# A fused attention and FFN kernel on one core: the opening phase rebuilt, steps spread by time, the global values product in one matmul

## The chip, the core and the metric

The kernel runs on one NeuronCore of one Trainium2 chip. The metric is the device time of one execution in microseconds (us); the time before is 426.11 us, the median of three runs (425.46 to 426.5). The engines are called as the profile calls them: PE is TensorE (matmuls; PEld is its weight load), DVE is VectorE, ACT is ScalarE, POOL is GpSimd, SP is SyncE. PE writes its results to PSUM[...]; DVE and ACT read them from there into SBUF. DMAs are issued from SP and from POOL. Each engine runs its own instructions in the order in which the program issues them, and waits for the other engines by semaphores.

## The reference

Eight batches of eight heads, 576 tokens, 64 values a head. Attention with a window of 32 tokens to each side and eight global tokens that see, and are seen by, every token; then a gated FFN over all 4608 tokens:

```python
scores = scale * np.matmul(q, k.transpose(0, 1, 3, 2))
mask = (np.abs(pos[:, None] - pos[None, :]) <= 32) | is_global[:, None] | is_global[None, :]
attn = softmax(np.where(mask, scores, -1e9))            # over the last axis
x = np.matmul(attn, v).transpose(0, 2, 1, 3).reshape(4608, 512)
g = x @ w_gate                                          # 512 -> 1536
out = (g * sigmoid(g) * (x @ w_val)) @ w_out            # 1536 -> 512
```

All inputs and the output are float32 in HBM; inside the kernel the matmuls take bf16.

## The kernel before

**Attention of one batch** (`attention(b)`) is a list of sixteen small groups of steps. `step_T(hp)` transposes keys and queries of two heads on PE (lines 274 to 296), ACT copies the keys from PSUM to `kT`, DVE the queries to `qT`. `step_GT` transposes the gathered global rows (`kqm`). `step_S2` and `step_SG` are the scores of the global queries and of the global keys, with the mask tables `mg2` and `mg` multiplied in on DVE; `step_P2T` and `step_AV2` give the result rows of the global queries, which DVE turns into the operand `gvt`. `step_S(u)` computes the scores of a band of 128 keys by 64 queries for two or four heads, ACT takes the exponential (line 396), DVE multiplies by `band` (line 401). `step_AV(u)` multiplies the probabilities by the values, for two blocks of 128 tokens: into each PSUM tile `ps_av` go a global part (line 427) and eight local products of 64 queries each (line 437). The local products of the odd half blocks need `vb`, a copy of the values moved by 64 partitions, which SP makes by two DMAs from `va` to `vb` (lines 97 to 101). `normalise` (lines 408 to 417, three DVE instructions) divides by the sum and writes `xa`. `step_X(tp)` transposes `xa` back, and ACT copies the result to `xT`, the FFN's input.

**The FFN** (`ffn(c)`) goes by chunks of 512 tokens, nine in all. `gate(fc)`, twelve times, makes two groups of four matmuls into the PSUM tiles `pg` and `pv` (line 525), a tanh on ACT (line 531), and two products on DVE (lines 533 and 536), the last of which writes `h`. `outp(ts)`, four times, makes twelve matmuls into `po` (line 541); ACT scales it to `osb`, and SP stores that.

**The order of the work** is written out by hand. First come the loads and tables, then the whole of `attention(0)`, then nine chunks; after the i-th of the sixteen units of chunk c stands the i-th group of `attention(c+1)`. After the third unit stands `prefetch(c+2)`: gather, queries and keys, values and `gather_mask` of a later batch, all issued by POOL. POOL's queue at the start is: keys and queries of heads 0 to 3, constants, heads 4 to 7, more constants and clears of `va`, the gather, the five value loads, `gather_mask(0)`, six loads of gate and value weights (512 KB each as written), `prefetch(1)`, four loads of the output weights.

**PSUM**: tag `sc` (two banks, one buffer) holds scores; tag `m` (two buffers of one bank) holds `ps_t`, `ps_g`, `ps_p2t`, `ps_av`, `ps_x`; tag `f` (four buffers of one bank) holds `pg`, `pv`, `po`.

Of the kernel before, what the change touches and what calls it, by code (L numbers as in the profile page):

```python
# [17 lines left out]
P = 128  # L18
# [8 lines left out]
def kernel(  # L27
# [22 lines left out]
    NCH = NT // CH  # L50
# [23 lines left out]
    def load_qk_part(b, tiles, hg):  # L74
        for name, src in (("k", k), ("q", q)):
            nc.gpsimd.dma_start(  # L76
                out=tiles[name][:, 4 * hg : 4 * hg + 4, :],
                in_=src[b, 4 * hg : 4 * hg + 4].rearrange("h (p j) d -> p h (j d)", j=LJ),
            )
# [6 lines left out]
    va_bufs = [const.tile([P, 5, H, W], BF16, name=f"va{i}") for i in range(2)]  # L86

    def load_v(b):
        va = va_bufs[b % 2]
        vs = v[b].rearrange("h s d -> s h d")  # L90
        for u in range(5):
            lo = WIN if u == 0 else 0
            hi = P - WIN if u == 4 else P
            t0 = P * u - WIN
            nc.gpsimd.dma_start(out=va[lo:hi, u, :, 0:D], in_=vs[t0 + lo : t0 + hi])  # L95

    def load_vb(b):
# [11 lines left out]
    load_qk_part(0, loaded[0], 0)  # L109
# [4 lines left out]
    iq_i = const.tile([P, KC], I32)  # L114
    nc.gpsimd.iota(iq_i, pattern=[[1, KC]], base=-WIN, channel_multiplier=0)
    load_qk_part(0, loaded[0], 1)
    i8_i = const.tile([P, NG], I32)
    nc.gpsimd.iota(i8_i, pattern=[[1, NG]], base=0, channel_multiplier=0)
    bofs_i = const.tile([P, B], I32)
    nc.gpsimd.iota(bofs_i, pattern=[[H * S, B]], base=0, channel_multiplier=0)  # L120
    band = const.tile([P, 64], BF16)
    nc.gpsimd.memset(band, 1.0)
    nc.gpsimd.affine_select(
        out=band, in_=band, compare_op=ALU.is_ge, fill=0.0,
        base=0, pattern=[[-1, 64]], channel_multiplier=1,
    )
    nc.gpsimd.affine_select(
        out=band, in_=band, compare_op=ALU.is_ge, fill=0.0,
        base=2 * WIN, pattern=[[1, 64]], channel_multiplier=-1,
    )  # L130
    for i in range(2):
        nc.gpsimd.memset(va_bufs[i][:, :, :, D : D + 2], 0.0)
        nc.gpsimd.memset(va_bufs[i][:, :, :, D : D + 1], 1.0)
        nc.gpsimd.memset(va_bufs[i][0:WIN, 0, :, :], 0.0)
        nc.gpsimd.memset(va_bufs[i][P - WIN : P, 4, :, :], 0.0)


    gidx_f = const.tile([P, NG], FP32)
    nc.vector.tensor_copy(
        out=gidx_f, in_=gidx_i64.bitcast(I32).rearrange("p (a b) -> p a b", b=2)[:, :, 0]  # L140
# [4 lines left out]
    )  # L145
    tmp8 = const.tile([P, NG], FP32)
# [3 lines left out]
    oh16 = const.tile([P, HP, 2, 2], FP32)  # L150
    nc.vector.tensor_reduce(
        out=oh16.rearrange("p h a r -> p (h a r)"),
        in_=ident.rearrange("p (a g) -> p a g", g=NG), axis=AX.X, op=ALU.add,
    )
    dmask = const.tile([P, HP, 2], FP32)
    nc.vector.tensor_tensor(out=dmask, in0=oh16[:, :, 0, :], in1=oh16[:, :, 1, :], op=ALU.add)
    mka = const.tile([P, 2, 2], FP32)
    nc.vector.tensor_reduce(
        out=mka, in_=oh16.rearrange("p h a r -> p a r h"), axis=AX.X, op=ALU.add
    )  # L160
    asel = const.tile([P, 2], FP32)
    nc.vector.tensor_reduce(out=asel, in_=mka, axis=AX.X, op=ALU.add)
    i8_f = const.tile([P, NG], FP32)
    nc.vector.tensor_copy(out=i8_f, in_=i8_i)
# [9 lines left out]
    bofs_f = const.tile([P, B], FP32)  # L174
    nc.vector.tensor_copy(out=bofs_f, in_=bofs_i)
    nc.vector.tensor_scalar(out=gofs, in0=bofs_f, scalar1=hrow, scalar2=None, op0=ALU.add)

# [21 lines left out]
    kqms = [None] * B  # L199
    g0 = gather(0)  # L200
    load_v(0)
    kqms[0] = gather_mask(*g0)
# [14 lines left out]
    for i in range(3):  # L217
        load_wgv(i)


    iq = const.tile([P, KC], FP32)
    nc.vector.tensor_copy(out=iq, in_=iq_i)
    nc.vector.tensor_scalar(out=iq, in0=iq, scalar1=gcol, scalar2=None, op0=ALU.subtract)
    m1 = const.tile([P, KC], BF16)
    nc.vector.tensor_scalar(out=m1, in0=iq, scalar1=0.0, scalar2=None, op0=ALU.is_equal)
    m0 = const.tile([P, KC], BF16)
    nc.vector.tensor_tensor(out=iq, in0=iq, in1=iq, op=ALU.mult)
    nc.vector.tensor_scalar(
        out=m0, in0=iq, scalar1=(WIN + 0.5) ** 2, scalar2=None, op0=ALU.is_gt
    )  # L230
    ones = const.tile([P, P], BF16)
    nc.vector.memset(ones, 1.0)
    ps_i = psc.tile([P, 2, 512], FP32, tag="sc", name="ps_i")
    for i in range(2):
        nc.tensor.matmul(
            out=ps_i[:, i, 0:320], lhsT=ones, rhs=m1[:, 320 * i : 320 * (i + 1)],
            start=True, stop=True,
        )
    mg = const.tile([P, S], BF16)
    mt = const.tile([P, KC], BF16)  # L240
    nc.vector.tensor_scalar(
        out=mg, in0=m0[:, WIN : WIN + S], scalar1=asel[:, 0:1], scalar2=None, op0=ALU.mult
    )
    nc.vector.scalar_tensor_tensor(
# [324 lines left out]
    for s in attention(0):  # L569
        for f in s:  # L570
            f()
# [40 lines left out]
```

The softmax here doesn't subtract the row's maximum and nothing guards it: scores larger than these inputs give would overflow.

## Time and profile before

| What | Value |
|---|---|
| Median of three runs | 426.11 us |
| The profiled execution, its own time | 426.5 us |
| Its span from first to last instruction | 424.5 us |
| PE busy | 377.0 us, 89% of the span |
| DVE busy | 266.2 us, 63% |
| ACT busy | 178.7 us, 42% |
| POOL busy | 92.7 us, 22% |
| First matmul of the first FFN chunk | 43.95 us |
| First matmul of the second chunk | 91.61 us |
| From chunk to chunk, second to seventh | 44.46 us |
| First matmul of the eighth chunk (no attention left) | 358.38 us |

Busy time is summed over instructions of an engine; the idle time before an instruction is put down to what released it. The modelled end of a matmul lies some tenths of a microsecond behind the time at which the next may start, so that distances between starts are the better measure on PE. The span is cut into three: the opening to 43.95 us, seven chunks that carry the attention of the next batch, and two chunks of FFN alone.

### The profile page before, as it was taken

The numbers are of one execution on the slowest core, as the hardware profiler recorded it, in microseconds if no ns is written. First come the engines' busy times: TensorE is split into PE (matmuls) and PEld (weight loads), VectorE is DVE, ScalarE is ACT, GpSimd is POOL, SyncE is SP. The second block draws the span as 40 slices with busy tenths as digits, with TensorE's granted clock in tenths as the row PEclk, the third lists the DMA queues.
The fourth block names the chain that finished last, engine by engine and source line by source line (L and its number), as shares of the span: only waits on it lengthen the run. The fifth ranks groups of instructions, "written<-read, shape, count | busy, mean of one in ns | idle before, by whom it ended". The sixth has DMA issues, their size and how long they took to land.

```text
span 424.5 us, 9105 instructions
## 1 busy us (share of the span) xinstructions
PE 377.0 (89%) x3788; PEld 192.4 (45%) x3850; DVE 266.2 (63%) x583; ACT 178.7 (42%) x281; POOL 92.7 (22%) x134
## 2 busy tenths in 40 slices
PE   0467888999989998999899989999999989999996
PEld 0345444444544444454454445445444544444442
DVE  5456488727872788267845795488628882761760
ACT  1153255345643464256524653356245633323321
POOL 8942848232015101312113211100000000000000
PEclk9999999999999999999999999999999999999999
DMA  7999999883537273647355726500030002002002
GB/s 112 68 199 208 183 212 149 109 142 57 82 23 123 73 110 23 100 92 113 23 76 116 112 18 71 124 2 2 27 121 6 2 2 100 0 2 99 0 2 99
DMA packets 62234, 33.76 MB, mean 80 GB/s; under 512 B 39409, under 2 KB 56305, under 8 KB 62193
## 3 DMA queue, kind: packets, MB, share of 16 engines
q0 software_dynamic: 55584, 19.40, 40.6%
q1 hardware_dynamic: 6608, 13.77, 9.7%
q8 instruction: 30, 0.49, 0.5%
q14 instruction: 12, 0.09, 0.1%
HBM read 38.28 MB, written 9.44 MB: 112 GB/s over the span
## 4 chain that ended last, share of the span: by engine, by line
PE 69%; DVE 19%; ACT 5%; issue 3%; POOL 2%; DVEq 0%; ACTq 0%; POOLq 0%
PE po L541 22%; PE pg L525 17%; PE pv L525 16%; DVE pt L401 5%; PE ps_t L282 5%; DVE xa L414 3%; DVE h L536 3%; DVE gv L533 3%; ACT pe L396 3%; PE ps_x L468 2%; DVE den L413 2%; PE ps_av L427 1%; ACT kT L288 1%; DVE gvt L365 1%; PE ps_av L437 1%
## 5 line engine op out<-in xcount | busy, mean ns | idle before, releaser
L533 DVE SCALAR_TENSOR_TENSOR gv<-th,pg 128x512 bf16<-128x512 bf16 x108 | 74.0, 685 | 61.4 <-ACT th L531 54.4
L525 PE MATMUL pv<-xT,wv_sb 128*128 128x512 bf16 x418 | 109.7, 381 | 0.4
L525 PE MATMUL pg<-xT,wg_sb 128*128 128x512 bf16 x400 | 106.7, 382 | 3.4 <-issue 2.6
L541 PE MATMUL po<-wo_sb,h 128*128 128x512 bf16 x416 | 97.3, 380 | 0.8
L531 ACT ACTIVATE th<-pg 128x512 bf16<-128x512 f32 x108 | 64.5, 598 | 69.3 <-PE pg L525 65.0
L536 DVE TENSOR_TENSOR h<-gv,pv 128x512 bf16<-128x512 bf16 x108 | 74.3, 688 | 11.9 <-PE ps_s L388 0.5
L525 PEld LDWEIGHTS <-wv_sb 128*128 128x128 bf16 x432 | 42.5, 98 | 51.6 <-issue 1.1
L541 PEld LDWEIGHTS <-h 128*128 128x128 bf16 x432 | 40.2, 98 | 45.3
L95 POOL DMA_DIRECT2D va<-in_v_dram x40 | 33.8, 852 | 122.6 <-PE ps_av L437 90.4
L546 ACT ACTIVATE osb<-po 128x512 f32<-128x512 f32 x36 | 21.5, 597 | 89.5 <-PE po L541 89.5
L525 PEld LDWEIGHTS <-wg_sb 128*128 128x128 bf16 x432 | 36.1, 98 | 38.2 <-issue 4.1
L396 ACT ACTIVATE pe<-ps_s 128x1024 bf16<-128x1024 f32 (+1 forms) x40 | 37.6, 940 | 15.4 <-PE ps_s L388 13.9
L410 DVE TENSOR_REDUCE den<-ps_av 128x4 f32<-128x8 f32 x72 | 11.5, 159 | 41.1 <-PE ps_av L457 34.4
L288 ACT COPY kT<-ps_t 128x576 bf16<-128x576 bf16 x32 | 20.4, 638 | 36.8 <-PE ps_t L282 36.8
L401 DVE TENSOR_TENSOR pt<-pe,band 128x1024 bf16<-128x1024 bf16 (+1 forms) x40 | 25.4, 635 | 11.2 <-ACT pe L396 11.1
L414 DVE TENSOR_TENSOR xa<-ps_av,den 128x256 bf16<-128x256 f32 x72 | 30.6, 425 | 2.5
L293 DVE COPY qT<-ps_t 128x576 bf16<-128x576 bf16 x32 | 24.0, 750 | 4.5 <-PE ps_t L282 4.5
L427 PE MATMUL ps_av<-gvt,pg 128*64 128x264 bf16 x128 | 19.1, 305 | 6.3 <-DVE xa L414 3.3
L474 ACT COPY xT<-ps_x 128x512 bf16<-128x512 bf16 x32 | 18.0, 588 | 15.1 <-PE ps_x L468 15.1
L76 POOL DMA_DIRECT2D k_bf<-in_k_dram x16 | 11.8, 735 | 38.8 <-PE ps_t L282 35.5
L437 PEld LDWEIGHTS <-pt 128*64 128x64 bf16 x512 | 18.8, 117 | 0.3
L468 PE MATMUL ps_x<-ident,xa 128*128 128x128 bf16 x128 | 12.3, 231 | 7.5 <-DVE xa L414 7.2
(93 smaller groups left out, 286.6 us busy)
## 6 DMA issues: line engine op xcount, KB each, us to landing
out_dram<-osb SPq DMA_DIRECT2D x36, 256.0 KB, 2.0
k_bf<-in_k_dram POOLq DMA_DIRECT2D x16, 288.0 KB
q_bf<-in_q_dram POOLq DMA_DIRECT2D x16, 288.0 KB
vb<-va SPq DMA_DIRECT2D x16, 264.0 KB, 4.0
va<-in_v_dram POOLq DMA_DIRECT2D x24, 128.0 KB
va<-in_v_dram POOLq DMA_DIRECT2D x16, 96.0 KB
wg_sb<-in_moe_w_gate_dram POOLq DMA_DIRECT2D x3, 512.0 KB
wv_sb<-in_moe_w_val_dram POOLq DMA_DIRECT2D x3, 512.0 KB
```

The source lines that it names most:

```text
L95: nc.gpsimd.dma_start(out=va[lo:hi, u, :, 0:D], in_=vs[t0 + lo : t0 + hi])
L288: nc.scalar.copy(out=kT[:, hp, WIN : WIN + S].rearrange("p (i j) -> p i j", j=LJ), in_=ps.rearrange("p j i -> p i j"),)
L293: nc.vector.tensor_copy(out=st["qT"][:, hp, :].rearrange("p (i j) -> p i j", j=LJ), in_=ps.rearrange("p j i -> p i j"),)
L396: nc.scalar.activation(out=pe, in_=ps[:, :, 0 : 64 * ns].rearrange("p r (s c) -> p r s c", c=64), func=AF.Exp, scale=SCALE,)
L401: nc.vector.tensor_tensor(out=pt.rearrange("p r s c -> p (r s) c"), in0=pe.rearrange("p r s c -> p (r s) c"), in1=bc(band, [[0, 2 * ns], [ ...
L414: nc.vector.tensor_tensor(out=xa, in0=ps[:, :, 0:D], in1=den.to_broadcast([P, 4, D]), op=ALU.mult)
L427: nc.tensor.matmul(out=ps[64 * e : 64 * e + 64], lhsT=st["pg"][:, P * tp + 64 * e : P * tp + 64 * e + 64], rhs=st["gv"].rearrange("p h r c ...
L525: nc.tensor.matmul(out=ps, lhsT=w[:, cc, P * fc : P * (fc + 1)], rhs=xT[:, cc, t0 : t0 + CH], start=(cc == 0), stop=(cc == NCC - 1),)
L531: nc.scalar.activation(out=th, in_=pg, func=AF.Tanh, scale=0.5)
L533: nc.vector.scalar_tensor_tensor(out=gv, in0=th, scalar=1.0, in1=pg, op0=ALU.add, op1=ALU.mult)
L536: nc.vector.tensor_tensor(out=st["h"][:, fc, :], in0=gv, in1=pv, op=ALU.mult)
L541: nc.tensor.matmul(out=po, lhsT=st["h"][:, fc, P * ts : P * (ts + 1)], rhs=wo_sb[:, fc, :], start=(fc == 0), stop=(fc == NFC - 1),)
```

## The change

Five things are changed at once.

1. **Opening.** Keys and queries are issued first; the constants that the gather needs come next, and the gather follows at once. The clears of `va` and `kT` move from POOL to DVE. The values of batch 0 are loaded by SP as float32 into `vst` (which shares a buffer with `h`), after a dependency on the first keys and queries, and POOL copies them to `va` as bf16. The weight loads go between: one pair before `gather_mask(0)`, one before the copies, one behind. The output weights now stand ahead of `prefetch(1)`. The mask tables are made in `tables()`, which squares on ACT.
2. **Banks.** The first eighteen tiles of tag `m` in batch 0 take a buffer of tag `f` two times out of three.
3. **Start of the FFN.** Of `attention(0)`, the steps up to the first two `step_X` (`head`) run alone. The other seven groups (`rest`) go into chunk 0, and chunk 0 is two halves of 256 tokens.
4. **Spreading.** `interleave` places the groups by the summed weights of the units (1.73 a gate of 512 tokens, 2.6 an `outp`) in place of one after each unit; `prefetch` is a group of its own ahead of `attention(c+1)`.
5. **Global part.** The two matmuls of 64 queries in `step_AV` become one of 128.

```diff
@@ opening, POOL's and SP's queues
+    first = load_qk_part(0, loaded[0], 0)
+    ones = const.tile([P, P], BF16)
+    nc.vector.memset(ones, 1.0)
+    for i in range(2):
+        nc.vector.memset(va_bufs[i][:, :, :, D : D + 2], 0.0)
...
+        nc.vector.memset(kT_bufs[i][:, :, WIN + S : KC], 0.0)
...
-    kqms = [None] * B
-    g0 = gather(0)
-    load_v(0)
-    kqms[0] = gather_mask(*g0)
+    vst = hpool.tile([P, 5, H, D], FP32, tag="h", name="vst")
+    vs0 = v[0].rearrange("h s d -> s h d")
+    for u in range(5):
+        lo, hi, t0 = v_block(u)
+        ins = nc.sync.dma_start(out=vst[lo:hi, u], in_=vs0[t0 + lo : t0 + hi])
+        if u == 0:
+            for f in first:
+                tc.add_manual_dep(
...
+    kqms = [None] * B
+    g0 = gather(0)
+    load_wgv(0)
+    band = const.tile([P, 64], BF16)
...
+    kqms[0] = gather_mask(*g0)
+    load_wgv(1)
+    for u in range(5):
+        lo, hi, t0 = v_block(u)
+        for a, z in ((lo, 64), (64, hi)) if u == 0 else ((lo, hi),):
+            nc.gpsimd.tensor_copy(out=va_bufs[0][a:z, u, :, 0:D], in_=vst[a:z, u])
+    load_wgv(2)
@@ tables
+    def tables():
+        nc.scalar.activation(out=iq, in_=iq, func=AF.Square, bias=ngcol, scale=1.0)
+        m1 = work.tile([P, KC], BF16, tag="p2", name="m1")
+        nc.vector.tensor_scalar(out=m1, in0=iq, scalar1=0.25, scalar2=None, op0=ALU.is_lt)
+        ps_i = psc.tile([P, 2, 512], FP32, tag="sc", name="ps_i")
+        for i in range(2):
+            nc.tensor.matmul(
+                out=ps_i[:, i, 0:320], lhsT=ones, rhs=m1[:, 320 * i : 320 * (i + 1)],
+                start=True, stop=True,
+            )
+        nc.vector.tensor_scalar(
+            out=mt, in0=iq, scalar1=sgn[:, 1:2], scalar2=thr[:, 1:2],
+            op0=ALU.mult, op1=ALU.is_gt,
+        )
...
+        nc.vector.scalar_tensor_tensor(
+            out=mg2.rearrange("p (i c) -> p i c", i=2), in0=ps_i[:, :, 0:320], scalar=thi,
+            in1=mt.rearrange("p (i c) -> p i c", i=2), op0=ALU.is_lt, op1=ALU.mult,
+        )
+        nc.vector.tensor_scalar(
+            out=mg, in0=iq[:, WIN : WIN + S], scalar1=sgn[:, 0:1], scalar2=thr[:, 0:1],
+            op0=ALU.mult, op1=ALU.is_gt,
+        )
@@ attention
+        def mtile(shape, dt, name):
+            cnt[0] += 1
+            if b == 0 and cnt[0] <= FIRST_M and cnt[0] % 3:
+                return pf.tile(shape, dt, tag="f", name=name)
+            return pm.tile(shape, dt, tag="m", name=name)
...
-                ps = pm.tile([P, 4, W], FP32, tag="m", name="ps_av")
-                for e in range(2):
-                    nc.tensor.matmul(
-                        out=ps[64 * e : 64 * e + 64],
-                        lhsT=st["pg"][:, P * tp + 64 * e : P * tp + 64 * e + 64],
-                        rhs=st["gv"].rearrange("p h r c -> p (h r) c")[:, 4 * hg : 4 * hg + 4, :],
-                        start=True, stop=False, skip_group_check=True,
-                    )
+                ps = mtile([P, 4, W], FP32, "ps_av")
+                nc.tensor.matmul(
+                    out=ps, lhsT=st["pg"][:, P * tp : P * (tp + 1)],
+                    rhs=st["gv"].rearrange("p h r c -> p (h r) c")[:, 4 * hg : 4 * hg + 4, :],
+                    start=True, stop=False, skip_group_check=True,
+                )
...
+        if b == 0:
+            head = [
+                L(step_T, 0), L(step_T, 1), tables, L(step_S, 0), L(step_T, 2), L(step_T, 3),
+                L(step_GT), L(step_S2), L(step_SG), vb, L(step_P2T), L(step_S, 1),
+                L(step_AV2), L(step_AV, 0), L(step_AV, 1), L(step_X, 0), L(step_X, 1),
+            ]
+            rest = [
+                [L(step_S, 2)], [L(step_S, 3)], [L(step_AV, 2)],
+                [L(step_AV, 3), L(step_S, 4)], [L(step_X, 2), L(step_X, 3)],
+                [L(step_AV8)], [L(step_X8)],
+            ]
+            return head, rest
@@ ffn(c) becomes ffn(t0, n): n columns in gate, n // P outputs
-        return [L(gate, fc) for fc in range(NFC)] + [L(outp, ts) for ts in range(4)]
+        return [(n / CH * 1.73, L(gate, fc)) for fc in range(NFC)] + [
+            (2.6, L(outp, ts)) for ts in range(n // P)
+        ]
@@ main loop
+    def interleave(units, steps):
+        total = sum(d for d, _ in units)
+        t = 0.0
+        i = 0
+        for d, f in units:
+            f()
+            t += d
+            while i < len(steps) and (i + 0.5) * total <= t * len(steps):
+                for g in steps[i]:
+                    g()
+                i += 1
+        assert i == len(steps)
+    head, rest = attention(0)
+    for f in head:
+        f()
+    for c in range(NT // CH):
+        steps = rest
+        rest = []
+        if c + 2 < B:
+            steps.append([lambda c=c: prefetch(c + 2)])
+        if c + 1 < B:
+            steps += attention(c + 1)[1]
+        units = ffn(0, 256) + ffn(256, 256) if c == 0 else ffn(CH * c, CH)
+        interleave(units, steps)
```

## The prediction

> **What bounds it now.** I read the page first, then PE's waits by stage, then the order of time on PE, ACT and POOL. From the page's slices:
>
> ```profile
> PE   0467888999989998999899989999999989999996
> DMA  7999999883537273647355726500030002002002
> ```
>
> PE is full from about the fifth slice on; only the opening is thin, and there the DMA engines are full. PE's waits before 43.9 us, then in the third chunk (136.24 to 180.7):
>
> ```profile
> PE ps_i L235 <- DVE ones L232: 10.4, 1, 10.4
> PE ps_g L302 <- POOL kqm L193: 5.8, 1, 5.8
> ```
> ```profile
> PE ps_x L468 <- DVE xa L414: 0.8, 2, 0.5
> PE ps_g L302 <- ACT kT L288: 0.5, 1, 0.5
> ...
> PE ps_av L427 <- DVE gvt L373: 0.3, 1, 0.3
> PE ps_av L427 <- DVE xa L414: 0.3, 1, 0.3
> ```
>
> Six chunks of 44.46 us are bound by PE, with some 2 us of waiting each: what lengthens PE's queue there counts six times. POOL's order of time:
>
> ```profile
> 10.88 1.04 POOL L183 DMA_INDIRECT kg<-in_k_dram,gofs  x1 [0.17 <-DVE mg L241]
> ...
> 31.98 0.70 POOL L76 DMA_DIRECT2D q_bf<-in_q_dram  x1 [5.02 <-DMA wv_sb<-in_moe_w_val_dram]
> ...
> 42.25 3.42 POOL L95 DMA_DIRECT2D va<-in_v_dram  x4 [1.86 <-DMA wv_sb<-in_moe_w_val_dram]
> ```
>
> The weights come at one 512 KB load in 2.5 us (210 GB/s in the stage 34 to 36). The view of the tile `vb` ends:
>
> ```profile
> DMA to landing us min/median/max: 3.4/4.0/10.1
> ```
>
> The 10.1 is batch 0's, issued at 20.36 with weights queued. Last, PE from an output group into `step_AV` and back:
>
> ```profile
> 170.39 0.81 PE L541 MATMUL po<-wo_sb,h 128*128 128x512 bf16 x3
> 171.13 0.30 PE L427 MATMUL ps_av<-gvt,pg 128*64 128x264 bf16 x2
> 171.26 0.19 PE L437 MATMUL ps_av<-va,pt 128*64 128x66 bf16 x1
> ...
> 171.39 0.28 PE L427 MATMUL ps_av<-gvt,pg 128*64 128x264 bf16 x2
> ...
> 171.73 0.82 PE L541 MATMUL po<-wo_sb,h 128*128 128x512 bf16 x3
> ```
>
> Three matmuls of 0.216 from 170.39 end at 171.03, so 0.10 passes before the first 128x64 matmul. The two global matmuls take 0.13 together, so they run side by side; a tile takes 0.24 to 0.26. The second ends at 171.63, and 0.10 passes again.
>
> **The Trainium skill.** "TensorEngine Tiling (Array Packing)", Key Properties: changing the tiling mode drains TensorE; the trace's 0.10 agrees. "TensorE: Matmul & The Clock Gate", Part 1: after idling the array runs at half speed until about 3.4 us of work. The trace agrees: twelve transposes start 0.6 before their followers at 21.47 and 0.28 before at 50.43, and the FFN's matmuls are slow for 3 us from 43.95. "DMA: Bandwidth & Descriptors", Issuing engines are not separate DMA queues: SP's and POOL's transfers share the same engines and interleave; `vb`'s 10.1 agrees.
>
> **The change, part by part.**
>
> *Opening.* `gofs` needs `ident` (POOL, 3.52) and ten small DVE operations of 0.2 to 0.4: 5.9. The gather is then issued at 5.9, not 10.88. The clears now on DVE (2 to 3 us, by the rows of DVE's memsets) run before `ident` is there and cost nothing. The tables take 3 to 4 us of DVE and a Square on ACT, which is not in the trace: by "ScalarE: Activation LUTs", What ACT_TABLE_LOAD costs, an estimate of 280 ns + 640 x 0.833 = 0.81. PE's chain at its slow clock (four T pairs at 1.2, tables, S0, GT, S2, SG, P2T, S1, AV2, with the ACT and DVE rows of before between them) would reach AV0 at 24 to 26. Six banks spare the T pairs waits of some 0.2 each. All this costs or gains nothing, because the values come later; without that cover AV0's 24 to 26 would be the bound.
>
> The values: of keys and queries, 0.59 MB have moved at 6.7 (70 to 200 GB/s from 3 us on), so SP's waiting first DMA goes at about 7.3; behind it on SP stand the other four, then `vb`. The rest of the keys and queries moves until 10.0. Two weight pairs, issued by POOL before 15, are 2.1 MB: 10.2 at 205 GB/s. The values alone took 5.0 (stage 15 to 20). If all share evenly the values land last, 25.2; going first they land at 15. I take 25, since `vb` too waited behind weights. POOL waits for each block and copies it: no such copy is in the trace; between the 0.40 of a product of 128 elements and four times that, six copies, all but the last under the loads: +0.8 (uncovered, +5). Behind the copies stand the last weight pair, the output weights and `prefetch(1)`. `vb`: issue 0.5 and the median 4.0, as few weights are queued then: 30.5 (with 10.1: 36). AV0 and AV1 at the slow clock, normalising 0.74 a tile, two transposes, one copy: 5.2. **The FFN starts at about 36**, not at 43.95.
>
> *Chunk 0* takes over seven groups of batch 0. A gate of 256 columns is 8 x 0.108 = 0.87 on PE; on DVE one 128x256 row (L414) is 0.42, two dependent ones 0.87. Both are even, and all attention comes on top on both.
> - First twelve gates: DVE starts 1.45 late and idles 1.4 more in the slow phase; 12 x 0.87 + 5.2 for pt and normalising = 15.7; the last h is there at +18.5. An output needs that only for its twelfth matmul, so PE goes on at +17.3.
> - Two outputs, 5.2. Behind the first stand T0, GT, T1 together, behind the second T2, T3. From batch 1 on there are two banks again: each pair waits for kT (0.64) and qT (0.75), behind `osb` (0.60) on ACT: 2.5 and 2.1. That makes 27.1.
> - Second twelve: DVE 12 x 0.87 + 7.3 = 17.8, starting 1.0 late; PE goes on at +45.9.
> - Two outputs, 5.2; AV3, X2, X3 in a row with 1.3 of waiting for xa (2.4), AV8, X8 with 0.95 (1.6): **55.1**.
>
> Before it was 47.66. So chunk 1 starts at 36 + 55.1 = 91.1, against 91.61: **-0.5**. The other loads, moved one after another at the rate above, land before they are asked for: weights by 34 (45), output weights by 42 (53), batch 1's keys by 48 (56). `vst` has `h`'s buffer, but the copies are done at 26.
>
> *Global part.* The array time is the same 0.11. But 128x128, then 128x64, twice, is new: AV0 and AV1, which follow a 64x128 score, have five changes of mode for two; AV2 and AV3 have two more each. 10 x 0.10 = 1.0 a batch.
>
> *Spreading*, chunks 1 to 5 (17 groups): by the weights nothing stands behind gate 8; S1 with AV2, S2 with AV0, S3 with AV1 stand behind gates 9, 10, 11; X0, X1, S4 and AV2 fall together behind the first output, and X2, X3 and AV8 behind the third. DVE gets 1.7 us of room before S1, so the waits that PE's starts show (0.36 for gvt, 0.45 and 1.17 for xa) shrink, I work out, to 0.26, 0 and 0.2: -1.5. But AV2 must have X0's bank, and X0's copy stands behind `osb`:
>
> ```profile
> 174.53 0.60 ACT L546 ACTIVATE osb<-po 128x512 f32<-128x512 f32 x1 [2.70 <-PE po L541]
> 175.02 1.07 ACT L474 COPY xT<-ps_x 128x512 bf16<-128x512 bf16 x2
> ```
>
> `osb` starts 0.21 behind PE's last matmul, xT 0.49 later, and the bank is free at 0.21 + 0.49 + 0.58 + 0.04 = 1.32. AV2 would be ready at 0.87 to 0.97: with its second tile +0.4. AV8 is ready at 0.55: +0.77, and the fourth output and the next chunk's gates stand behind it. With 1.0 of mode changes: -1.5 + 0.4 + 0.77 + 1.0 = **+0.65 a chunk, 3.2 for five**. Chunk 6 has sixteen groups, X0 and X1 again behind a gate: the changes in AV0 and AV1 vanish in DVE's waits, 0.4 remain, and AV8's 0.77: **+1.2**. `prefetch` goes one group earlier; POOL is a chunk ahead there (its longest waits are for `ps_av`): nothing.
>
> The sum: -0.5 + 3.2 + 1.2 = +3.9. The span becomes 428.4, the profiled execution 430.4 with the 2.0 around it; since that stood 0.4 above the median, **430.0**.
>
> **Rivals.**
> A. *The values go first.* For: `vb`, once it moved (stages 26 to 28, 323 and 253 GB/s), pushed the weights aside. Against: the six us that it stood before. Each us is one for the FFN, down to PE's own chain, a start at 30 to 31. It decides from a landing at 20: start 31, chunk 1 at 86.1, the whole 426.1 - 5.5 + 4.4 = 425.0; with less cost of spreading down to 421. This is the end on the faster side.
> B. *Mode changes are hidden* under waits or preloaded weights: 5 x 1.0 + 0.4 less, 424.6 to 426. Against: 0.10 on both sides of every AV.
> C. *DVE bounds chunk 0.* Four `f` banks hold two gates, so two normalises in a row stop PE, and DVE cannot catch up under the outputs: +3 a half, 436. For: 0.87 against 0.87. Against: DVE is idle under outputs now.
>
> **How the numbers follow.** Main case 0.46 (427.5 to 434), A 0.26 (421 to 425), B 0.10, C or a later landing 0.18 (434 to 440). The range 422 to 437 leaves out A's best and C's worst. No change is within 0.3% (1.3 us), about what a measurement of this kernel can tell. Faster: A and a part of B, less A's slow edge, 0.26; same: the rest of B and that edge, 0.13; slower: 0.61.
>
> **What would show it.** Right: the FFN's first pg near 36, with va, `vb` and AV on the chain before it; the values landing near 25; chunk 1 at 91; DVE near full in chunk 0; later chunks of 45.1, the wait of X for xa gone, one of 0.8 for ACT's xT before AV8, and 0.1 between the 128x264 and the 128x66 matmuls. Wrong: the FFN by 31, chunks of 44.4 or less, or PE waiting for a load of batch 1.

## The result, and the profile after

The changed kernel takes **437.26 us** (median of four runs, 436.12 to 438.54), beside 425.78 us of the kernel before (four runs): a ratio of 1.0271, 95% interval 1.0234 to 1.0308. Slower was forecast, but by 3.9 us; it is 11.5. The profiled execution took 436.75 us, its span is 435.0 (before 426.5 and 424.5).

| First matmul of | before | after | after less before |
|---|---|---|---|
| AV0 of batch 0 | 30.88 | 30.72 | -0.16 |
| the FFN (chunk 0) | 43.53 | 37.40 | -6.13 |
| chunk 1 | 91.61 | 96.45 | +4.84 |
| chunk 7 | 358.38 | 368.25 | +9.87 |
| end of the span | 424.5 | 435.0 | +10.5 |

Two of these starts are read from the weight loads, because some records of matmuls are missing from a trace. In the profile before, the first group of the FFN shows three matmuls of four:

```profile
43.95 1.49 PE L525 MATMUL pg<-xT,wg_sb 128*128 128x512 bf16 x3 [0.22 <-issue]
```

The weights of the missing one were loaded at 43.42, and matmuls of this group start 0.427 apart, so that the FFN began at 43.53 and chunk 0 took 48.08; the 43.95 and 47.66 that stand ahead of the prediction and in it are 0.42 off. Chunk 1 was not touched by that. In the kernel after it is the first matmul of chunk 1 that has no record; its weights were loaded at 96.45.

So chunk 0 became 10.97 us longer (59.05 for 48.08), which is more than the earlier start gains. The next six chunks give 5.03 more: five of 45.22 and one of 45.69, for 44.46. The last 0.6 lies behind the last output: from the last `osb` to the end of the span it is 4.34 us, before 3.71.

The page's slices, as shown of before:

```profile
PE   2618889789999999899998999899989999999995
DMA  8989999353736371746166434800030001002002
```

PE starts earlier, in the first slice, but it is thin there, and the DMA engines are full for the first seven slices (before, they were nearly full for nine). PE's waits up to 37.4 us (in total, times, longest), then POOL's order of time (start, duration, what, idle time before it) and the last line of the view of `vb`:

```profile
PE ps_av L388 <- POOL va L258: 8.0, 2, 4.2
PE ps_t L312 <- DMA k_bf<-in_k_dram: 5.8, 1, 5.8
...
PE ps_av L465 <- DMA vb<-va: 1.2, 1, 1.2
PE ps_av L456 <- DVE gvt L403: 1.1, 1, 1.1
```
```profile
15.92 2.48 POOL L258 CAST va<-vst 32x512 bf16<-32x512 f32 x4
24.14 0.61 POOL L258 CAST va<-vst 128x512 bf16<-128x512 f32 x1 [5.73 <-DMA vst<-in_v_dram]
28.65 0.61 POOL L258 CAST va<-vst 96x512 bf16<-96x512 f32 x1 [3.90 <-DMA vst<-in_v_dram]
29.21 0.75 POOL L235 DMA_DIRECT2D wg_sb<-in_moe_w_gate_dram  x1
```
```profile
DMA to landing us min/median/max: 3.1/3.7/6.8
```

PE's first wait, 10.4 us for the tables, is now one of 5.8 for the first keys (2.3 for a table follows), and the 5.8 for `kqm` is gone; in its place PE waits 8.0 for the values. The last values are there at 28.65, and the first gate, 37.40, follows from that: their copy takes 0.61, `vb` 3.2, and from the first use of `vb` in AV0 to the copy of X1 it is 4.9.

PE's waits in chunk 0 (37.3 to 96.4), then in the third chunk (141.6 to 186.9), which answers to the one shown of before:

```profile
PE ps_x L496 <- DVE xa L444: 3.1, 6, 0.9
PE ps_x L507 <- DVE xa L444: 1.5, 2, 0.9
PE ps_av L456 <- DVE gvt L403: 1.4, 1, 1.4
```
```profile
PE ps_av L477 <- ACT xT L502: 0.7, 1, 0.7
PE ps_g L332 <- ACT kT L318: 0.5, 1, 0.5
PE ps_av L456 <- ACT xT L502: 0.4, 1, 0.4
```

In chunk 0 PE waits 6.0 us for DVE's `xa` and `gvt`, where before it was 1.8, by the same view from 43.9 to 91.6:

```profile
PE ps_x L468 <- DVE xa L414: 0.8, 2, 0.5
PE ps_av L427 <- DVE xa L414: 0.7, 2, 0.4
PE ps_av L427 <- DVE gvt L373: 0.3, 1, 0.3
```

In the third chunk X no longer waits for `xa`; AV8 and AV2 wait for ACT's `xT` instead. How that comes about stands in ACT's and PE's order of time at the third output:

```profile
182.69 0.60 ACT L592 ACTIVATE osb<-po 128x512 f32<-128x512 f32 x1 [2.92 <-PE po L587]
183.19 1.07 ACT L502 COPY xT<-ps_x 128x512 bf16<-128x512 bf16 x2
```
```profile
182.50 0.61 PE L496 MATMUL ps_x<-ident,xa 128*128 128x128 bf16 x8
183.82 0.30 PE L477 MATMUL ps_av<-gvt,pg 128*64 128x264 bf16 x2 [0.71 <-ACT xT L502]
```

X's transposes start at 182.50, ACT scales the output until 183.29 and copies xT only behind that, and AV8, which needs X's bank, starts 1.32 behind X: to the hundredth the 1.32 that the prediction worked out for a bank to come free.

### The profile page after: what moved, and what is told of

It reads as the page before. It is cut to its first block, busy times and chain, and to the rows that moved or that the text cites. A ratio compares the mean times of both kernels' runs of the same rounds, so it can differ in the third digit from the quotient of the medians.

```text
span 435.0 us, 9259 instructions
## 1 busy us (share of the span) xinstructions
PE 383.9 (88%) x3826; PEld 201.9 (46%) x3882; DVE 266.7 (61%) x611; ACT 179.8 (41%) x294; POOL 87.8 (20%) x127
## 3 DMA queue, kind: packets, MB, share of 16 engines
q0 software_dynamic: 50896, 18.81, 37.3%
q1 hardware_dynamic: 11296, 14.95, 11.5%
## 5 line engine op out<-in xcount | busy, mean ns | idle before, releaser
L568 PE MATMUL pg<-xT,wg_sb 128*128 128x512 bf16 (+1 forms) x458 | 112.2, 362 | 3.2 <-issue 1.3
L568 PE MATMUL pv<-xT,wv_sb 128*128 128x512 bf16 (+1 forms) x468 | 112.9, 361 | 0.4
L576 DVE SCALAR_TENSOR_TENSOR gv<-th,pg 128x512 bf16<-128x512 bf16 (+1 forms) x120 | 75.8, 632 | 58.7 <-ACT th L574 55.2
L574 ACT ACTIVATE th<-pg 128x512 bf16<-128x512 f32 (+1 forms) x120 | 66.5, 555 | 77.9 <-PE pg L568 71.3
L580 DVE TENSOR_TENSOR h<-gv,pv 128x512 bf16<-128x512 bf16 (+1 forms) x120 | 76.1, 634 | 12.6 <-DVE gv L576 0.2
L568 PEld LDWEIGHTS <-wg_sb 128*128 128x128 bf16 x480 | 41.7, 99 | 39.6 <-issue 4.6
L440 DVE TENSOR_REDUCE den<-ps_av 128x4 f32<-128x8 f32 x72 | 11.4, 159 | 35.7 <-PE ps_av L485 22.3
L456 PE MATMUL ps_av<-gvt,pg 128*128 128x264 bf16 x64 | 18.4, 288 | 5.8 <-DVE gvt L403 3.7
L465 PEld LDWEIGHTS <-pt 128*64 128x64 bf16 x512 | 13.6, 112 | 17.9 <-issue 11.9
L465 PE MATMUL ps_av<-vb,pt 128*64 128x66 bf16 x256 | 20.6, 203 | 1.2 <-DMA vb<-va 1.2
L312 PE MATMUL ps_t<-ident,k_bf 96*64 96x96 bf16 x384 | 15.2, 219 | 6.3 <-DMA k_bf<-in_k_dram 5.8
```

The source lines that it names most:

```text
L465: nc.tensor.matmul(out=ps[64 * e : 64 * e + 64, hl, :], lhsT=pt[:, hl % 2, slot, :], rhs=vv[:, tp, 4 * hg + hl, :], start=False, stop=(hl ...
L568: nc.tensor.matmul(out=ps[:, 0:n], lhsT=w[:, cc, P * fc : P * (fc + 1)], rhs=xT[:, cc, t0 : t0 + n], start=(cc == 0), stop=(cc == NCC - 1),)
L574: nc.scalar.activation(out=th[:, 0:n], in_=pg[:, 0:n], func=AF.Tanh, scale=0.5)
L576: nc.vector.scalar_tensor_tensor(out=gv[:, 0:n], in0=th[:, 0:n], scalar=1.0, in1=pg[:, 0:n], op0=ALU.add, op1=ALU.mult,)
L580: nc.vector.tensor_tensor(out=st["h"][:, fc, 0:n], in0=gv[:, 0:n], in1=pv[:, 0:n], op=ALU.mult)
```

## The experiments

All ratios are to the kernel before on the same chip, with 95% intervals; they are not quotients of the medians. "FFN" is the first gate's start, "chunk 1" that of the second chunk, "later chunks" the distance from start to start behind it. In g1, s1 and o5 the first matmul of the FFN has no record, as in the kernel before; its start is taken 0.427 ahead of the second.

| Run | Median us | Ratio | FFN | chunk 1 | later chunks |
|---|---|---|---|---|---|
| after | 437.26 | 1.0271 (1.0234 to 1.0308) | 37.40 | 96.45 | 45.22 |
| g1 | 427.93 | 1.0085 (1.0064 to 1.0105) | 44.01 | 90.54 | 44.91 |
| s1 | 426.96 | 1.0054 (1.0033 to 1.0074) | 43.52 | 90.78 | 44.70 |
| g2 | 433.88 | 1.0246 (1.0205 to 1.0288) | 37.01 | 95.13 | 44.70 |
| s2 | 434.06 | 1.0224 (1.0207 to 1.0241) | 37.57 | 96.45 | 44.90 |
| h1 | 436.09 | 1.0224 (1.0191 to 1.0258) | 47.95 | 95.80 | 45.22 |
| h2 | 438.55 | 1.0310 (1.0270 to 1.0349) | 49.24 | 99.63 | 45.22 |
| v1 | 427.70 | 1.0077 (1.0040 to 1.0114) | 28.24 | 87.22 | 45.22 |
| v2 | 428.31 | 1.0068 (1.0050 to 1.0085) | 29.18 | 87.92 | 45.23 |
| o2 | 430.26 | 1.0101 (1.0079 to 1.0124) | 37.00 | 95.29 | 44.46 |
| o3 | 420.17 | 0.9897 (0.9858 to 0.9935) | 37.95 | 84.70 | 44.45 |
| o4 | 421.93 | 0.9922 (0.9905 to 0.9938) | 36.48 | 86.47 | 44.45 |
| o5 | **417.40** | 0.9826 (0.9808 to 0.9844) | 36.80 | 82.63 | 44.46 |

### The steady chunks: one matmul, and the spreading (g1, g2, s1, s2)

Each of the two parts was done alone on the kernel before and taken out of the kernel after. g1 is before with the one matmul:

```diff
-                for e in range(2):
-                    nc.tensor.matmul(
-                        out=ps[64 * e : 64 * e + 64],
-                        lhsT=st["pg"][:, P * tp + 64 * e : P * tp + 64 * e + 64],
...
+                nc.tensor.matmul(
+                    out=ps, lhsT=st["pg"][:, P * tp : P * (tp + 1)],
...
```

> The kernel before with one edit: the two global matmuls of 64 queries become one of 128. Theory M (each change of tiling mode drains PE for 0.10 us): ps_av tiles take 0.46 us of PE for 0.26; in the order of before the six changes of AV0 and AV1 vanish in the waits for DVE that stand behind them, four stay: +0.4 us a chunk, 44.9 for 44.46, and the whole +3 us (1.007). If nothing is covered: 45.5 a chunk, +8 us (1.019). Rival (changes are free or preloaded): 44.5 a chunk, 1.000.

Chunks of 44.91: +0.45. PE in AV0 of g1, by order of time:

```profile
157.87 0.27 PE L426 MATMUL ps_av<-gvt,pg 128*128 128x264 bf16 x1 [0.26 <-DVE gvt L373]
158.07 0.22 PE L435 MATMUL ps_av<-va,pt 128*64 128x66 bf16 x1
...
158.32 0.29 PE L426 MATMUL ps_av<-gvt,pg 128*128 128x264 bf16 x1
```

From the global matmul to the first local one it is 0.20, 0.09 more than the 0.11 of array time, and a tile takes 0.45 instead of 0.24 to 0.26. The change of mode is there in every tile of the later chunks (0.20 to 0.22), but the waits of X and AV2 for `xa`, 1.1 in the third chunk of before, are 0.6 here: part of the longer queue fills them. The trace doesn't tell whether the array drains or the weights make PE wait: the local products' weights start to load at 158.07, with their first matmul, where between matmuls of one form they are loaded ahead.

g2 is the kernel after with that edit turned round:

```diff
-                nc.tensor.matmul(
-                    out=ps, lhsT=st["pg"][:, P * tp : P * (tp + 1)],
...
+                for e in range(2):
+                    nc.tensor.matmul(
+                        out=ps[64 * e : 64 * e + 64],
+                        lhsT=st["pg"][:, P * tp + 64 * e : P * tp + 64 * e + 64],
...
```

> The changed kernel with one part undone: the global part again as two matmuls of 64 queries side by side. Theory M: the changed kernel's order leaves little wait for DVE behind AV, so most of 1.0 us comes back in each of seven chunks: chunks 1 to 6 at 44.5 for 45.3, the whole 6 to 8 us below the changed kernel, 1.009 to 1.013 of before. Rival (free): as the changed kernel, 1.027.

Chunks of 44.70 against 45.22: in the order of the kernel after the one matmul costs 0.52. The expectation, most of 1.0 a chunk and a ratio of 1.009 to 1.013, is missed: the ratio is 1.0246, and it is nearer to its rival. So the changes of mode cost about half of what was put down for them in either order.

s1 is the kernel before with part 4 alone, `prefetch` as a group of its own included:

```diff
-        for i, f in enumerate(ffn(c)):
-            f()
-            if i < len(steps):
-                for g in steps[i]:
-                    g()
...
+        units = [(1.73 if i < NFC else 2.6, f) for i, f in enumerate(ffn(c))]
+        interleave(units, steps)
```

> The kernel before with one edit: groups spread by time, prefetch as a group of its own, in all chunks. Theory: X0's wait for xa goes (about -1.5 us a chunk at most), waits for X's banks come before AV2 (0.4) and AV8 (0.7), some wait for DVE stays: 44.3 to 44.8 a chunk for 44.46, 0.998 to 1.004. Rival (the order is what makes the later chunks slower): 45.3 a chunk, 1.012.

Chunks of 44.70, and 45.23 for the last one with attention in it. PE's waits in its third chunk:

```profile
PE ps_av L449 <- ACT xT L474: 0.7, 1, 0.7
...
PE ps_av L427 <- DVE xa L414: 0.3, 1, 0.3
PE ps_av L427 <- ACT xT L474: 0.2, 1, 0.2
```

The wait for `xT` before AV8 comes from the spreading alone. Of the waits of before, X's 0.8 is gone and AV2's 0.3 stays; +0.24 is left, within the 44.3 to 44.8 that were expected (the ratio, 1.0054, is just above the 0.998 to 1.004). The last chunk's +0.77 is the price that the prediction put on AV8's bank.

s2 is the kernel after with the order of before from chunk 1 on:

```diff
     for c in range(NT // CH):
+        if c:
+            steps = attention(c + 1)[1] if c + 1 < B else []
+            for i, (d, f) in enumerate(ffn(CH * c, CH)):
+                f()
+                if i < len(steps):
+                    for g in steps[i]:
+                        g()
+                if i == 2 and c + 2 < B:
+                    prefetch(c + 2)
+            continue
...
```

> The changed kernel with the old order of one group behind each unit from chunk 1 on; chunk 0 stays. Theory: chunks 1 to 6 become those of the kernel before with one global matmul, 44.9 us, for 45.3: 2.5 us below the changed kernel, 1.021 of before. Rival (the order is what costs): 44.5, 5 us below, 1.015.

Chunks of 44.90, as expected: the spreading costs 0.32 in the kernel after. Alone the two parts cost 0.45 and 0.24, together 0.76: over six chunks they make 5.0 of the 10.5 us. Chunk 1 starts at 96.45 here too: chunk 0 is a matter by itself.

### Chunk 0: halves and seven groups (h1, h2)

h1 takes part 3 back:

```diff
     head, rest = attention(0)
-    for f in head:
+    for f in head + [g for s in rest for g in s]:
         f()
+    rest = []
...
-        units = ffn(0, 256) + ffn(256, 256) if c == 0 else ffn(CH * c, CH)
+        units = ffn(CH * c, CH)
```

> Leaves the halves out: the whole of attention(0) runs before the FFN, and chunk 0 is one of 512 tokens; all else as in the kernel after. Theory H (half gates are too short to cover the chains ACT, DVE, PE, and the seven groups of batch 0 cost as much inside the chunk as ahead of it, or more): the FFN starts 7 to 8 us later (44.5 to 45.5), chunk 0 takes 46.5 to 48, chunk 1 starts at 91.5 to 93 instead of 96.45, the whole is 3.5 to 5 us faster than the kernel after: 432 to 434, a ratio to the kernel before of 1.014 to 1.019. Rival (the seven groups and the slow clock cost the same anywhere, and the halves cost nothing): chunk 1 at 96 to 97, ratio 1.026.

The FFN starts 10.5 us later, not 7 to 8, chunk 0 takes 47.85 as expected, and chunk 1 starts at 95.80, 0.65 earlier than in the kernel after and not at 91.5 to 93. That is near the rival: taken at its word the halves would cost hardly anything. But two things differ ahead of the FFN. PE waits 3.5 us for `vb` (1.2 in the kernel after), so that X1 ends 1.8 later; and the seven groups alone, with no gates between them, are long. h2 takes the two apart: it is h1 with the halves put back.

```diff
-        units = ffn(CH * c, CH)
+        units = ffn(0, 256) + ffn(256, 256) if c == 0 else ffn(CH * c, CH)
```

> The kernel after with the whole of attention(0) before the FFN, as in h1, but with chunk 0 in two halves of 256 tokens: the halves alone, without the seven groups of batch 0 in them. Chunk 0 takes 47.85 in h1 and 59.05 in the kernel after. Theory D (half gates leave chains of ACT, DVE and PE uncovered): 49.5 to 51.5, so that the seven groups are some 8 to 9.5 of the 11.2. Rival 1 (halves cost nothing by themselves): 47.8 to 48.4, all of the 11.2 is the seven groups. Rival 2 (halves are the main cost): 54 or more.

PE's order of time in h1 (the end of X1, where the seven groups begin, and the two chunk starts), then in h2:

```profile
38.20 0.61 PE L418 MATMUL ps_s<-qT,kT 64*128 64x64 bf16 x16
...
47.95 1.91 PE L568 MATMUL pg<-xT,wg_sb 128*128 128x512 bf16 x4
...
95.80 1.03 PE L568 MATMUL pg<-xT,wg_sb 128*128 128x512 bf16 x4
```
```profile
49.24 1.06 PE L568 MATMUL pg<-xT,wg_sb 128*128 128x256 bf16 x4
...
99.63 1.03 PE L568 MATMUL pg<-xT,wg_sb 128*128 128x512 bf16 x4
```

Halves alone: 99.63 - 49.24 = 50.39, within the 49.5 to 51.5 expected and 2.54 more than 47.85. The seven groups then add 59.05 - 50.39 = 8.66 inside chunk 0; ahead of the FFN they take 47.95 - 38.20 = 9.75. Placing them in the chunk saves 1.1, cutting the chunk to make that possible costs 2.5, and the first gate of the kernel after has to wait 0.94 for the copy of X1, which nothing covers. So all of the +4.84 at chunk 1 is told:

- AV0: -0.16.
- AV0 to X1 and the seven groups, 6.68 + 8.66 = 15.34, where the kernel before takes 12.65 for all of it: +2.69. The 0.94 and 1.2 for `vb` are in it.
- Halves: +2.54.
- Chunk 0 of 512 with one matmul and spreading, 47.85 for 48.08: -0.23.

Together 4.84. The terms rest on one profile each, and such stretches vary: the FFN of h1 and h2, equal up to there, starts 1.3 apart, and chunk 0 as one of 512 tokens takes from 45.8 (o5) to 48.1 (before) among these kernels. One cause can be read from the starts. PE is at half speed when the FFN begins, and how long that lasts is not the same: in h1 the groups start 1.71 apart up to 53.07, in h2 0.85 apart only up to 51.80. The groups lose 2.7 us by it in h1 and in the kernel after, 1.6 in h2. With the same loss everywhere the halves would cost some 3.6 and the seven groups some 7.6 inside the chunk (estimates from these starts). Of the halves' 2.54 the size is sure by about one only; the sign is sure, for the intervals of h1 and h2 do not overlap, and their ratios are some 3.7 us apart.

### The values and what stands ahead of them (v1, v2)

v1 issues the weights behind POOL's copies:

```diff
     g0 = gather(0)
-    load_wgv(0)
...
-    load_wgv(1)
     for u in range(5):
         ...
             nc.gpsimd.tensor_copy(out=va_bufs[0][a:z, u, :, 0:D], in_=vst[a:z, u])
-    load_wgv(2)
+    for i in range(3):
+        load_wgv(i)
```

> All three pairs of gate and value weights are issued behind POOL's copies of the values. Theory V (weights in front of the values hold them): the last values land at 15 to 16, the copies end by 18, vb lands near 22, the FFN starts at 29 to 30.5, and the time is 6 to 8 us below the kernel after: a ratio to the kernel before of 1.008 to 1.013. Rival 1 (the values of 256-byte runs are slow by themselves): the last values land beyond 20, a gain of 3 us at most. Rival 2 (the weights become what is late): the FFN starts by 31, but its gates wait for weights, and chunk 1 starts later than 90.

POOL's order of time, PE's at AV0, and the landing of `vst`:

```profile
14.21 3.41 POOL L256 CAST va<-vst 32x512 bf16<-32x512 f32 x5
19.01 0.61 POOL L256 CAST va<-vst 96x512 bf16<-96x512 f32 x1 [1.39 <-DMA vst<-in_v_dram]
```
```profile
23.26 0.38 PE L455 MATMUL ps_av<-gvt,pg 128*128 128x264 bf16 x1 [1.94 <-DVE gvt L402]
...
28.24 1.01 PE L567 MATMUL pg<-xT,wg_sb 128*128 128x256 bf16 x4 [0.67 <-ACT xT L501]
```
```profile
DMA to landing us min/median/max: 5.6/6.9/7.5
```

The slowest value load takes 7.5 us where it took 15.1 with two weight pairs beside it (the last one, whose landing is not recorded, some 16.5 until its copy starts), and the copies end at 19.6 instead of 29.3. The values land at 19.0, later than the 15 to 16 expected and within its rival's 20. AV0 starts 7.5 earlier, at PE's and DVE's own pace, the FFN 9.2 earlier. The gates do not wait for weights. (v1's nine times lie between 426.44 and 431.80, wider than the others.)

How the weights hold the values back is in the trace of the kernel after. From 19 to 25 us POOL's queue carries weights (the first line) and SP's the values (the second); packets, MB and the share of time follow (shares of packets that overlap, so that they add up to more than the whole):

```profile
q0 software_dynamic: 940, 0.94, 91.9%
q1 hardware_dynamic: 933, 0.23, 29.8%
```

The two queues get the same number of packets, whatever their size: 1 KB for a weight, 256 bytes for a value. So the values get a fifth of the bytes as long as weights are queued beside them.

v2 lets POOL load the values straight into `va`, behind the gather and ahead of the weights; `vst` and the copies fall away:

```diff
     g0 = gather(0)
+    load_v(0)
     load_wgv(0)
...
-        ins = nc.sync.dma_start(out=vst[lo:hi, u], in_=vs0[t0 + lo : t0 + hi])
...
-            nc.gpsimd.tensor_copy(out=va_bufs[0][a:z, u, :, 0:D], in_=vst[a:z, u])
```

> Batch 0's values are loaded by POOL straight into va as bf16, behind the gather and ahead of the weights; no vst, no copies on POOL. Theory V: the last values land at 16 to 18, vb near 22 to 23, FFN from 29.5 to 31, a ratio to the kernel before of 1.008 to 1.013, as with the weights behind the copies. Rival: the wait is in the transfer itself, not in what stands ahead of it; then values land beyond 20 and the FFN starts no earlier than 34.

The FFN starts at 29.18, a little ahead of the 29.5 to 31 expected. On one queue the values keep their place ahead of the weights, and the weights may be issued early: PE does not wait for values. Both versions are still slower than the kernel before: chunk 0 is as long as in the kernel after (58.98 and 58.74), and the 5 us of the later chunks are untouched.

### The opening alone, and a version that beats both (o2 to o5)

o2 is v1 with parts 3, 4 and 5 taken back: two matmuls, groups by unit, all of `attention(0)` ahead of the FFN. Only the opening, the banks and the order of steps in `attention(0)` are left of the change.

```diff
     head, rest = attention(0)
-    for f in head:
+    for f in head + [g for s in rest for g in s]:
         f()
     for c in range(NT // CH):
-        steps = rest
...
-        interleave(units, steps)
+        steps = attention(c + 1)[1] if c + 1 < B else []
+        for i, (d, f) in enumerate(ffn(CH * c, CH)):
+            f()
...
```

> The kernel before with the new opening (banks included) and the weights behind the copies of the values; pairs of global matmuls, groups by unit, the whole of attention(0) before the FFN, chunk 0 of 512 tokens. If the early gather is worth what the page of before shows (5.8 us of PE's wait for kqm) and the values come by 18: the FFN starts at 36 to 38 instead of 43.95, chunk 0 takes 46 to 47.7, the chunks 44.46 each, and the ratio is 0.981 to 0.988. If the values still hold AV0 back to 28 or later, the FFN starts beyond 41 and the ratio is above 0.993.

The FFN starts at 37.00, as it should, but chunk 0 takes 58.29 and the ratio is 1.0101, not 0.981 to 0.988:

```profile
48.07 0.69 PE L311 MATMUL ps_t<-ident,k_bf 96*64 96x96 bf16 x12 [7.74 <-DMA k_bf<-in_k_dram]
```

Batch 1's keys are late, and behind the wait PE is slow: the granted clock is 0.50 from 43.3 to 57.0 us. The keys stand behind six weight loads and four loads of the output weights. In the kernel after, v1 and v2 the output weights stand ahead of them too, and it does no harm there: the T groups of batch 1 come behind the first twelve gates and an output, in the kernel after 22 us behind the first gate.

o3 puts those loads ahead of the output weights again:

```diff
+    prefetch(1)
     for i in range(4):
         nc.gpsimd.dma_start(
             out=wo_sb[:, 3 * i : 3 * i + 3, :],
...
-    prefetch(1)
```

> o2 with batch 1's loads ahead of the output weights again, as in the kernel before. If what made o2 slow is only that those loads stood behind the output weights (7.7 us of PE's wait for keys in chunk 0): FFN from 37, chunk 0 in 46 to 47.7, chunk 1 at 83 to 85, a ratio to the kernel before of 0.981 to 0.986. Rival: the gate and value weights, now issued late, hold those loads back in any order; then the wait for k_bf stays over 3 us and the ratio is above 0.99.

Chunk 0 takes 46.75, chunk 1 starts at 84.70, and no load is waited for, as expected; the ratio, 0.9897, is above the expected 0.981 to 0.986.

o4 sets attention(0)'s score groups S2, S3 and S4 between the value groups, as in the kernel before:

```diff
-                L(step_AV2), L(step_AV, 0), L(step_AV, 1), L(step_X, 0), L(step_X, 1),
+                L(step_AV2), L(step_S, 2), L(step_AV, 0), L(step_S, 3), L(step_AV, 1),
+                L(step_X, 0), L(step_X, 1), L(step_S, 4), L(step_AV, 2), L(step_AV, 3),
+                L(step_X, 2), L(step_X, 3), L(step_AV8), L(step_X8),
             ]
-            rest = [
...
+            rest = []
```

> o3 with attention(0)'s steps from AV2 on in the order of the kernel before (score groups S2, S3, S4 between the value groups). The waits for gvt (1.9), ACT's pe (1.1) and xa (0.8 and 1.6) shrink: the FFN starts at 34.5 to 36, 1 to 2.5 earlier than in o3, a ratio of 0.976 to 0.983. Rival: the first pair of weights is not there before 36; then the FFN's first gate waits for it and nothing is won against o3.

The FFN starts 1.47 earlier than in o3, at 36.48 and not by 36, and chunk 0 takes 49.99, so that the ratio is 0.9922 and not 0.976 to 0.983. PE at its start, then two stretches with their lengths: PE's busy time, the granted clock, and the share (summed over packets that overlap, so that it can exceed 1) and rate of the DMA engines:

```profile
39.83 0.45 PE L311 MATMUL ps_t<-ident,k_bf 96*64 96x96 bf16 x12
41.26 0.45 PE L311 MATMUL ps_t<-ident,q_bf 96*64 96x96 bf16 x12 [0.99 <-DMA q_bf<-in_q_dram]
42.36 0.59 PE L331 MATMUL ps_g<-ident,kqm 128*128 128x128 bf16 x2 [0.65 <-POOL kqm L207]
42.78 1.70 PE L563 MATMUL pg<-xT,wg_sb 128*128 128x512 bf16 x4
44.27 1.91 PE L563 MATMUL pv<-xT,wv_sb 128*128 128x512 bf16 x4
```
```profile
39.58:42.99 3.41, 1.65 (x29) 1.00 1.36 199
42.99:46.41 3.42, 3.42 (x16) 0.50 2.36 158
```

PE was at its full clock at 39.83. After two waits of 0.99 and 0.65 for batch 1's queries and `kqm` it is back at half: the second gate's groups take 1.49 from start to start (42.78 to 44.27) where 0.88 is usual, and the granted clock is 0.50 for 3.4 us. The Trainium skill, "TensorE: Matmul & The Clock Gate", HAM oscillation, tells of waits for a DMA that throttle TensorE again, so that the work behind them starts cold, and gives gaps of more than some 3.4 us as the rule. Here no gap was longer than 0.99; in the 3.41 us before the clock fell, PE was busy for 1.65. For this kernel the measurement decides. Chunk 0 is 3.2 longer than o3's: the waits make 1.6 of it and the half clock 1.7, but o3 in its turn was slow for longer at the start, so that some of the 3.2 is not accounted for.

o5 loads batch 1 behind the first weight pair, ahead of the other two:

```diff
-    for i in range(3):
-        load_wgv(i)
+    load_wgv(0)
...
     prefetch(1)
+    for i in range(1, 3):
+        load_wgv(i)
```

> o4 with batch 1's loads issued behind the first pair of gate and value weights, ahead of the other two pairs and the output weights. If o4's loss against o3 is the two waits for batch 1's keys in chunk 0 (0.99 and 0.65) and PE's slow clock after them: FFN at 36 to 37, no wait for a load in chunk 0, chunk 0 in 46 to 47.7, chunk 1 at 82.5 to 84.2, the chunks 44.46 each, a ratio to the kernel before of 0.981 to 0.987, below o3's 0.9897. Rival: the second or third pair of weights becomes late; then PE waits for weights behind the fourth or the eighth gate, chunk 1 starts beyond 85, and the ratio is 0.99 or more.

```profile
37.22 1.49 PE L562 MATMUL pg<-xT,wg_sb 128*128 128x512 bf16 x3 [0.22 <-issue]
38.50 1.55 PE L562 MATMUL pv<-xT,wv_sb 128*128 128x512 bf16 x4
39.99 0.45 PE L310 MATMUL ps_t<-ident,k_bf 96*64 96x96 bf16 x12
40.27 0.42 PE L310 MATMUL ps_t<-ident,q_bf 96*64 96x96 bf16 x12
```

No load is waited for in chunk 0, PE is at full speed from 40.0 on and stays there, chunk 0 takes 45.83, chunk 1 starts at 82.63, all as expected or a little better. At 417.40 us it is the fastest: 1.7% below the kernel before (1.6 to 1.9), and some 20 us below the kernel after. The new opening, so ordered, wins 9 us up to chunk 1 (82.63 for 91.61): 6.7 by the start of the FFN and 2.3 in chunk 0. Of the 2.3 about one may be the shorter slow phase of PE (an estimate: it ends some 2.8 us behind the first gate here and some 4.8 in the kernel before, and half of the difference is lost), and that phase differs between profiles. In the kernel after, this gain was hidden by the weights in front of the values; in o2 and o4, by the keys behind the weights.

## Why the prediction was right and wrong

Slower was right, and the start of the FFN, the steady chunks and the loads that are not waited for came out close. The size failed mainly in one term, chunk 0, by 4.0 us, in the steps "First twelve gates" and "Second twelve"; the start of the FFN adds 1.4, the later chunks 0.6, and 0.6 lies at the end.

*Opening: the FFN at 36, measured 37.40.* The cause was the one named: values behind two weight pairs, `vb` behind the values. The last value landed at 28.65, not 25.2; `vb` took 3.2, not 4.5. In the Trainium skill, "DMA: Bandwidth & Descriptors", Queues, rings and completion order, each DMA engine goes from queue to queue a packet at a time; the trace agrees, with 940 packets of one queue and 933 of the other, and so do the runs (15.1 us with weights on the other queue, 7.5 without, and in v2, where both are on one queue, no wait of AV2 for values at all). That the values land last, when the weights are through, was right; the time was not. The two queues moved 197 GB/s from 19 to 25 and not 205, the first load of `vb`, issued at 24.77, moved among the last values, and from 27 to 28.65 the DMA engines are nearly idle, with 0.08 MB moved, while a few last packets of values follow one another. Why these came so late stays open. PE's own chain, put at 24 to 26 for AV0, was too slow: v1 has it at 23.26. The Square on ACT, put at 0.81, took 0.83.

*Chunk 0: 55.1, measured 59.05.* The two outputs with T groups took 9.63 (forecast 9.8), the end 9.24 (9.2). The first twelve gates took 19.65 for 17.3, the second twelve 20.53 for 18.8. The prediction set both by DVE's sum of work and let PE follow it. DVE was not the bound: it was busy 13.59 of the 19.65 and 16.84 of the 20.53. PE is held by its own queue and its waits. In the first half these are some 14 us of gates and groups (12 x 0.87 and seven groups), 2.7 lost at the slow clock (six groups of four matmuls at 0.85 instead of 0.44, and 0.2 on S2), which lasted until 43.3, 5.9 us and not 3, and waits for `xa`, 1.9 by their view and more by the starts. (The 3 us were misread: in the trace of before the transposes from 47.08 still start 0.48 after one another, and the FFN had begun at 43.53. At 21.47 the prediction's 0.6 takes in short waits; 0.48, from 18.64 to 19.12, is the plain time.) In the second half it is some 17 and 2.7 of waits, the largest 1.41 for `gvt`: between AV2 and AV0 stand one gate of 0.87 and one score group, where a gate of 512 columns gives 1.73. Summing an engine's work was the mistake; what a half gate loses is cover for a chain through three engines. h2 shows the same without the seven groups: +2.54, with waits of 1.6 for ACT's `pe` and 0.8 for DVE's `gv` in chunk 0 that h1 does not have.

*Mode changes and spreading: +0.65 a chunk, measured +0.76; chunk 6 +1.2, measured +1.23.* The sum was right because two errors met. The mode changes were put at 1.0 and cost 0.45 to 0.52, as part of them fills waits. The spreading was put at -0.33 (waits spared 1.5, banks 0.4 and 0.77) and costs +0.24 alone: if the banks cost what was forecast, it spares only 0.9. That the two errors cancel is luck. The bank that AV8 waits for was right to the hundredth, and chunk 6 was right in its parts: the spreading alone costs 0.77 there (s1) and the matmul alone 0.44 (g1).

*The rivals.* A, the values first, had the whole at 425.0 with the FFN at 31. v1 makes that case: FFN at 28.24, and still 427.70, because chunk 0 was mis-sized in A too. B, hidden mode changes, is half true and of no help. C forecast 436 with 3 us in each half; that this is near is luck, for its mechanism is not there: in the kernel after no gate waits for an `f` bank (in h2 one waits 0.8 for DVE), and DVE has a third of the first half free.

*What was not seen.* The forecast had `vb` there at 30.5, and AV0 with it; the trace of before shows AV0 at 30.88:

```profile
30.88 0.43 PE L427 MATMUL ps_av<-gvt,pg 128*64 128x264 bf16 x2 [1.04 <-DVE gvt L373]
```

Side by side the two numbers say that the rebuilt opening wins nothing up to that point, so that all hangs on part 3, and part 3 was priced by DVE's sum. The earlier start of the FFN is work moved into chunk 0, where it is no cheaper: 15.34 for 12.65, by h2.

## What to carry to other kernels

When work is moved from in front of a loop into it, compare the whole to the first point that both versions share (here chunk 1), and price the pieces by PE's starts, waits included, not by the busiest engine's sum: halving a tile halves what hides a chain of ACT and DVE. What is needed first must not have a queue full of larger packets beside it: it goes ahead in the same queue, or the others are issued behind it; loads that an early start makes urgent (here batch 1's keys) have to move up with it. A matmul that saves instructions but brings a change of mode pays for it wherever PE's queue is full.

## What the runs showed of the hardware

- A half-speed phase of PE lasted 5.9 us from the start of the FFN in the kernel after, 5.3 in h1 and 3.3 in h2, two kernels that are equal up to there. In o4 two waits of 0.99 and 0.65 us brought half speed back for 3.4 us, in o2 one of 7.74 us for 13.7, counted from within the wait.
- Two DMA queues with work, POOL's weights in packets of 1 KB and SP's values in packets of 256 bytes, got 940 and 933 packets in the same 6 us: equal turns, and bytes as four to one.
- A cast from f32 to bf16 on POOL takes 0.61 us for 512 columns, on 32 partitions as on 128.
- Issuing the five value loads holds SP's queue for 6.33 us from 7.24 on (in h1 for 11.4, from 8.16 on). `vb`'s loads stand behind them, unharmed in the kernel after only because the values land later.
- The 0.6 us at the end of the span is there in all the kernels that load `vst` by SP (from the last chunk's start to the end about 35.7 us), and neither in v2, g1 and s1, which do not, nor in the kernel before (all about 35.05). Why an early load should lengthen the end stays open.
